# The opening of a two-layer SSM and GeGLU kernel: tap channels split 448 to 128 between TensorE and VectorE, D turned from one row, and two loads placed later

## Chip, cores and metric

The kernel runs on one core of one Trainium2 chip. The metric is the device time of one execution in microseconds (us). The kernel before takes 909.18 us, the median of three runs (909.0 to 909.36).

## What is computed

Four residual stages run over 2048 tokens of 576 channels: a gated convolution block (A), a GeGLU block (B), and the same two again with the same weights. All inputs are bf16.

```python
def _A_ref(q, k, v, shift_k, ssm_k, ssm_D):
    # k_shift: a causal convolution of k over 4 tokens, each channel with its 4 taps
    for t in range(ks):
        k_shift = k_shift + k_pad[:, t:t + S, :] * shift_k[:, ks - 1 - t][None, None, :]
    kv = k_shift * v
    # y: a causal convolution of kv over all 2048 tokens, each channel with its own filter ssm_k
    y = y + kv * ssm_D[None, None, :]
    return q * y

def _B_ref(x, w_gate, w_up, w_down):
    return (_gelu(x @ w_gate) * (x @ w_up)) @ w_down

x = A_q
x = x + _A_ref(_layernorm(x), A_k, A_v, A_shift_k, A_ssm_k, A_ssm_D)
x = x + _B_ref(_layernorm(x), B_w_gate, B_w_up, B_w_down)
x = x + _A_ref(_layernorm(x), ...)
x = x + _B_ref(_layernorm(x), ...)
```

## The kernel before

Tokens go in four blocks of 512, each held as 128 partitions by 4 rows (token 4p + i lies in partition p, row i). The long convolution is done block by block in a frequency domain: a block of kv is multiplied by tables of cosines and sines (W) on TensorE, the result (kc) is multiplied by the transformed filter (h0 and H) on VectorE, and the products (yb) go back through TensorE (L415). The term kv * D is folded into the filter: D is added to the filter's token 0. The GeGLU block streams its weights: wgu holds gate and up columns, wd the down rows, hT the hidden values. Its matmuls (L1743 and L1777) fill most of the time; the first of them, on half blocks, are at L1661.

All instructions are put out in an order written by hand or by a planner that runs at build time, and each engine works through its own list in that order. DMAs are issued from the lists of SP, ScalarE (ACT) and POOL; a DMA that waits holds up whatever is behind it in that list.

The function begin is the opening, for block 0. Around the change it does the following.

- sk9 and dv9 are the taps and D, loaded with 9 partitions of 64 channels each. L896 turns the taps into columns (wcol), L902 and L904 make diagonal matrices dg from them. L908 spreads the taps of the last 64 channels over all partitions (sx).
- L890 are matmuls on constants, eleven in all, before k has landed. L914 shifts the last three rows of k by one partition for the last 64 channels (kx).
- L922 turns k, four tiles of 128 channels (db 0 to 3, in two PSUM tiles, pts), and ScalarE copies them to kT (L927). shift_taps (L818) multiplies kT by the diagonals: fourteen matmuls for a pair of tiles. VectorE multiplies the result by v (L976).
- The remaining 64 channels (rest) are done by VectorE, multiply and add by tap (L938 to L944).
- L923 turns dv9, L931 copies it to dcol, and POOL adds dcol to the filter hn (L934). turn_h (L953) turns the filter, two of four rows at a time, rows 3 and 2 before the first taps and rows 1 and 0 before the second; L954 copies to hT0. Row 0 holds the token to which D is added.
- Then even and odd (L228) transform the filter, kfwd (L219) transforms v, apart (L233) and kacc (L359 to L362) are VectorE's work on both, straight (L415) is the way back, and the norm statistics of x stand between them. The transposes at L1461 and the copies at L1468 bring the normed x to the matmuls of L1661.
- POOL: taps_out writes the taps to DRAM as one row (skT) and loads k of block 1. At L1054 it loads that row into every partition as skc, the tap rows with which VectorE does the taps of blocks 1 to 3 (L194, L199, L204). At L1073 it loads v of block 1. Both are 576 KB. stats(3), the statistics of row 3, end with two POOL operations (L1484 and L1485). After them POOL works on L1229 and L1230 (norms), the stores of Hd and Kd (L425), additions by DMA (L389) and the loads of x_b (L1191) and kr (L547).
- SP loads, in this order: k, hn, v, W, x_b, Wx, W, the four turned pieces hx, wgu 0, the store Td, wgu 1 and wgu 2, hT1 (L966), and then three tiles of wd (L1186).

In first_half, L1667 is VectorE's multiplication of a hidden tile, and turn0 (L1461) turns rows 1 and 3 of x between the matmuls.

Of the kernel before, what the change touches and what calls it, by code (L numbers as in the profile page):

```python
# [15 lines left out]
ACT = mybir.ActivationFunctionType  # L16
ALU = mybir.AluOpType
F32 = mybir.dt.float32
BF16 = mybir.dt.bfloat16
# [3 lines left out]
P = 128  # L23
# [3 lines left out]
RT = BS // P  # L27
# [59 lines left out]
class Conv:  # L87
# [743 lines left out]
    def begin(self, head, tables):  # L831

        tc, nc, D, KS = self.tc, self.nc, self.D, self.KS
        nd = D // P
        width = lambda db: min(P, D - db * P)
        with ExitStack() as es:
            tmp = es.enter_context(tc.tile_pool(name="s_tmp", bufs=1))
            HP = P // 2
            NH = D // HP
            sk9 = tmp.tile([NH, 2, HP * KS], BF16, name="sk9")  # L840
            dv9 = tmp.tile([NH, 2, HP], BF16, name="dv9")
            sk9t = tmp.tile([NH, KS, HP], BF16, name="sk9t")
            hx = tmp.tile([P, RT, D], BF16, name="hx")
            dcol = tmp.tile([P, nd + 1], F32, name="dcol")
            nt = nd
            DW = D - nt * P
            wcol = tmp.tile([P, nt, KS], F32, name="wcol")
            sx = tmp.tile([P, KS, DW], BF16, name="sx")
            warm = tmp.tile([P, 1], F32, name="warm")
            self.Wx = tmp.tile([P, 2, P], BF16, name="Wx")  # L850
            Wn = tmp.tile([P, 2, P], BF16, name="Wn")
            hn = tmp.tile([P, nd + 1, BS], BF16, name="hn")
            hT0 = tmp.tile([P, RT, D], BF16, name="hT0")
            kT = head.scratch([P, nt, RT, P + 2], "kT")
            dg = head.scratch([P, nt, RT, P], "dg")
            kx = tmp.tile([P, RT + KS - 1, DW], BF16, name="kx")
            below = tmp.tile([P, P], BF16, name="below")
            wx = [tmp.tile([P, RT, DW], BF16, name=f"wx{i}") for i in range(2)]
            full = wx[1][:].rearrange("p i c -> p (i c)")[:, 0:256]

            twice = lambda src: src.unsqueeze(1).to_broadcast([NH, 2, src.shape[1]])
            nc.vector.memset(full, 1.0)
            nc.scalar.dma_start(out=sk9[:], in_=twice(self.sk.rearrange("(b p) j -> b (p j)", p=HP)))
            self.load_k(0, nc.sync)
            nc.scalar.dma_start(out=dv9[:], in_=twice(self.sD.rearrange("(b p) -> b p", p=HP)))
            nc.vector.memset(kT[:, :, :, 0:2], 0.0)
            nc.vector.memset(below[:, 0:1], 0.0)
            nc.vector.tensor_copy(out=below[:, 1:P], in_=self.ident[:, 0:P - 1])
# [16 lines left out]
            new_t = lambda: self.psp.tile([P, 2, 1024], BF16, tag="pr", name="pt")  # L885
            small_t = lambda: self.cpsp.tile([P, 2, 1024], BF16, tag="cps", name="cpt")

            def busy(ps, n):
                for _ in range(n):
                    nc.tensor.matmul(ps[:, 0, 0:256], lhsT=full[:, 0:P], rhs=full, start=True, stop=True)  # L890
            idle = small()
            busy(idle, 8)
            ps = new()
            halves = ((0, HP), (HP, P))
# [3 lines left out]
                nc.vector.tensor_copy(out=wcol[lo:hi], in_=ps[lo:hi, 0, 0:2 * nt * KS].rearrange("p (j b h) -> p b j h", b=nt, h=2)[:, :, :, h])  # L898

            def diagonals(db, js=range(KS)):  # L900
                for j in js:
                    nc.vector.tensor_scalar(out=dg[:, db, j, :], in0=self.ident[:], scalar1=wcol[:, db, j:j + 1], scalar2=None, op0=ALU.mult)  # L902
            for j in range(2):
                nc.scalar.activation(out=dg[:, nt - 1, j, :], in_=self.ident[:], func=ACT.Copy, scale=wcol[:, nt - 1, j:j + 1])  # L904
            for db in range(nt - 1):
                diagonals(db)
            ps = new()
            nc.tensor.matmul(ps[:, 0, 0:DW * KS], lhsT=self.ident[0:NH, NH - 1:NH].to_broadcast([NH, P]), rhs=sk9[:, 0, :], start=True, stop=True)  # L908
            nc.scalar.copy(out=sx[:], in_=ps[:, 0, 0:DW * KS].rearrange("p (d j) -> p j d", j=KS))
            busy(idle, 3)  # L910
            k, v = self.kt_[0], self.vt_[0]
            rest = slice(nt * P, D)
            px = new()
            nc.tensor.matmul(px[:, 0, 0:(KS - 1) * DW], lhsT=below[:], rhs=k[:, RT - KS + 1:RT, rest], start=True, stop=True)  # L914
            DBS = [(0, 1), (2, 3)]
            pts = []
            for n, dbs in enumerate(DBS):
                pt = new_t() if n else small_t()
                pts.append(pt)
                for e, db in enumerate(dbs):  # L920
                    for u in range(RT):
                        nc.tensor.transpose(pt[:, e, u * P:(u + 1) * P], k[:, u, db * P:(db + 1) * P], self.ident[:])  # L922
            nc.tensor.transpose(pt[:, 1, RT * P:RT * P + NH], dv9[:].rearrange("b h p -> b (h p)"), self.ident[0:NH, 0:NH])  # L923
            nc.scalar.copy(out=kx[:, 0:KS - 1, :], in_=px[:, 0, 0:(KS - 1) * DW].rearrange("p (i c) -> p i c", c=DW))
            for dbs, pt in zip(DBS, pts):
                ne = len(dbs)
                nc.scalar.copy(out=kT[:, dbs[0]:dbs[-1] + 1, :, 2:P + 2],  # L927
                               in_=pt[:, 0:ne, 0:RT * P].rearrange("p e (u q) -> p e u q", u=RT))
            for h, (lo, hi) in enumerate(halves):
                nb = (NH + 1 - h) // 2  # L930
                nc.scalar.copy(out=dcol[lo:hi, 0:nb], in_=pts[1][lo:hi, 1, RT * P + h:RT * P + NH:2])  # L931

            for lo, hi, w in ((0, nd, P), (nd, nd + 1, D - nd * P)):
                nc.gpsimd.tensor_tensor(out=hn[0:w, lo:hi, 0], in0=hn[0:w, lo:hi, 0], in1=dcol[0:w, lo:hi], op=ALU.add)  # L934

            tt = nc.vector.tensor_tensor
            tap = lambda j: sx[:, j, :].unsqueeze(1).to_broadcast([P, RT, DW])
            tt(out=wx[0][:], in0=k[:, 0:RT, rest], in1=tap(0), op=ALU.mult)  # L938
            nc.vector.tensor_copy(out=kx[:, KS - 1:, :], in_=k[:, 0:RT, rest])
            diagonals(nt - 1, range(2, KS))  # L940
            for j in range(1, KS):
                tt(out=wx[1][:], in0=kx[:, KS - 1 - j:KS - 1 - j + RT, :], in1=tap(j), op=ALU.mult)
                tt(out=wx[0][:], in0=wx[0][:], in1=wx[1][:], op=ALU.add)
            tt(out=v[:, :, rest], in0=wx[0][:], in1=v[:, :, rest], op=ALU.mult)  # L944

            def turn_h(pt, g):

                hv = hn[:].rearrange("p b (q i) -> p b i q", i=RT)
                for dbs in (range(nd), (nd,)):
                    for i in (2 * g + 1, 2 * g):  # L950
                        for db in dbs:
                            w = width(db)
                            nc.tensor.transpose(pt[:, i % 2, db * P:db * P + w], hv[0:w, db, i, :], self.ident[0:w, 0:w])  # L953
                nc.scalar.copy(out=hT0[:, 2 * g:2 * g + 2, :], in_=pt[:, :, 0:D])  # L954

            def taps_of(dbs, ps):
                o = ps[:].rearrange("p e (i c) -> p e i c", i=RT)
                for e, db in enumerate(dbs):
                    self.shift_taps(k, kT, dg, P, db, o[:, e])
                return o  # L960
            out = []
            for n, dbs in enumerate(DBS):
                turn_h(new_t(), 1 - n)
                out.append(taps_of(dbs, new() if n else small()))
            self.hT1 = head.scratch([P, RT, D], "hT1")[:]
            nc.sync.dma_start(out=self.hT1, in_=self.Td[1].rearrange("(p i) d -> p i d", i=RT))  # L966
            skT = tc.dram_tile([1, KS * D], BF16, name="skT")

            def taps_out():
                nc.gpsimd.tensor_copy(out=sk9t[:], in_=sk9[:, 0, :].rearrange("b (p j) -> b j p", j=KS))  # L970
                nc.gpsimd.dma_start(out=skT[:].rearrange("o (j b p) -> (o b) j p", j=KS, p=HP), in_=sk9t[:])
                self.load_k(1, nc.gpsimd)
            for dbs, o in zip(DBS, out):
                ne = len(dbs)
                vd = v[:, :, dbs[0] * P:(dbs[0] + ne) * P].rearrange("p i (e c) -> p e i c", e=ne)
                tt(out=vd, in0=o[:, 0:ne], in1=vd, op=ALU.mult)  # L976

            h0, kc, A, E = {}, {}, {}, {}
            self.H1 = head.stay()
# [21 lines left out]
            def kfwd(kt, s, ps):  # L1001
                if s == 0:
                    kc[kt] = self.kcp.tile([P, 2, D], BF16, tag="kc", name="kc")
                self.fwd_full(v, kt, s, kc[kt], ps=ps)
# [6 lines left out]
            def kacc(kt):  # L1011
                for part in range(2):
                    t = self.ybp.tile([P, D], BF16, tag="yb", name="yb")
                    self.prod(part, kc[kt], h0[kt], t[:])
                    A[(part, kt)] = t
# [35 lines left out]
            head.scales(0)  # L1051
            head.scales(2)
            kacc(0)
            nc.gpsimd.dma_start(out=self.skc[:].rearrange("p j d -> p (j d)"), in_=skT[:].broadcast_to([P, KS * D]))  # L1054
            kfwd(2, 0, small())
            kfwd(2, 1, new())
            even(1, 0)
# [12 lines left out]
            kfwd(3, 0, small())  # L1070
            head.even_out(2)
            kfwd(3, 1, new())
            self.load_v(1, nc.gpsimd)  # L1073
            head.act_stats(1)
            Y = {mt: new() for mt in (0, 2)}
            for kts in ((0, 2), (1,)):
# [26 lines left out]
            nc.scalar.activation(out=warm[:], in_=head.zero, func=ACT.Gelu_apprx_tanh)  # L1103
            self.keep_y(0, 3, Y[3])
            head.stats(3)
            head.gate(1, None, 0)
            self.A0 = A

# [762 lines left out]
```

## Time and profile before

| | us |
|---|---|
| runs, median (lowest to highest) | 909.18 (909.0 to 909.36) |
| the profiled execution | 909.58 |
| its span, first to last instruction | 907.8 |

Durations below come from this one profiled execution; it took 0.4 us more than the median, and 1.78 us of it lie outside the span. PE is TensorE's matmul, PEld its weight load, DVE VectorE, ACT ScalarE, SP the sync engine, whose list holds most DMA issues. Busy times of the engines in four stretches of the opening:

| stretch, us | PE | DVE | ACT | POOL | share of the DMA engines | GB/s |
|---|---|---|---|---|---|---|
| 0 to 13.4 | 11.78 | 8.15 | 7.93 | 1.03 | 0.92 | 286 |
| 13.4 to 28 | 14.12 | 13.91 | 12.10 | 8.13 | 1.04 | 272 |
| 28 to 34.5 | 5.82 | 5.68 | 4.00 | 0.00 | 1.07 | 284 |
| 34.5 to 50 | 15.37 | 14.76 | 10.45 | 10.15 | 1.10 | 304 |

The granted TensorE clock was 1.00 throughout. [...] Where an engine waited for several things, the profile names the one that came last, and that is an inference.

### The profile page before, as it was taken

How to read it: one execution, taken by the hardware profiler on the slowest of the kernel's cores; microseconds unless marked ns; L12 is line 12 of the kernel's file. 1: busy time of each engine (PE TensorE's matmuls, PEld its weight loads, DVE VectorE, ACT ScalarE, POOL GpSimd, SP SyncE). 2: the span in 40 equal slices, each digit the busy share in tenths (PEclk: the TensorE clock that was granted, in tenths of full speed). 3: DMA queues.
4: the chain of work that ended last, by engine and by line, in shares of the span. 5: the costliest groups of instructions: out<-in, count | busy, mean ns of one | idle time of the engine just before them, and what ended most of it. 6: DMA issues, size and time to landing. Idle time of an engine off the chain costs nothing.

```text
span 907.8 us, 19177 instructions
## 1 busy us (share of the span) xinstructions
PE 901.5 (99%) x8142; PEld 524.8 (58%) x8142; DVE 575.2 (63%) x988; ACT 328.3 (36%) x614; POOL 157.8 (17%) x336
## 2 busy tenths in 40 slices
PE   9999999999999999999999999999999999999998
PEld 6875646556466465564654655645646546556555
DVE  7989977688889884787898855443332335333332
ACT  6765455423222254443115133551121124321211
POOL 3324315120213031420104002310000003100000
PEclk9999999999999999999999999999999999999999
DMA  9999997766429319675815601961620621967620
GB/s 272 305 294 284 257 264 124 188 194 151 167 68 264 93 22 179 211 139 133 272 54 132 170 4 41 195 129 39 126 73 14 145 80 27 190 160 173 142 57 27
DMA packets 132076, 132.91 MB, mean 146 GB/s; under 512 B 46139, under 2 KB 123670, under 8 KB 131990
## 3 DMA queue, kind: packets, MB, share of 16 engines
q1 hardware_dynamic: 121728, 94.65, 46.5%
q0 software_dynamic: 10208, 37.02, 12.9%
q8 instruction: 63, 1.03, 0.5%
q14 instruction: 23, 0.19, 0.1%
q10 hardware_dynamic: 54, 0.01, 0.0%
HBM read 108.36 MB, written 12.39 MB: 133 GB/s over the span
## 4 chain that ended last, share of the span: by engine, by line
PE 96%; DVE 2%; DMA 1%; issue 0%; DVEq 0%; SPq 0%
PE gu L1743 59%; PE dn L1777 31%; PE gu L1661 2%; DMA hT<-Td 1%; PE cps L282 1%; PE ps L415 1%; PE ps L282 0%; PE cps L415 0%; DVE yb L362 0%; DVE prod L359 0%; DVE h L233 0%; DVE prod L361 0%; PE cps L890 0%; DVE hT L1667 0%; DMA out_dram<-ob 0%; PE cps L818 0%
## 5 line engine op out<-in xcount | busy, mean ns | idle before, releaser
L1743 PE MATMUL gu<-xnT,wgu 64*128 64x512 bf16 x4968 | 540.7, 376 | 0.0
L1743 PEld LDWEIGHTS <-wgu 64*128 64x128 bf16 x4968 | 239.7, 94 | 294.4 <-issue 6.2
L1752 ACT ACTIVATE ga<-gu 128x512 f32<-128x512 f32 x258 | 153.9, 597 | 450.9 <-PE gu L1743 442.5
L1753 DVE TENSOR_TENSOR hT<-ga,gu 128x512 bf16<-128x512 f32 x258 | 177.1, 686 | 200.4 <-ACT ga L1752 198.9
L1777 PE MATMUL dn<-wd,hT 128*128 128x288 bf16 x2304 | 292.1, 286 | 0.0
L1777 PEld LDWEIGHTS <-hT 128*128 128x128 bf16 x2304 | 223.5, 98 | 65.6 <-issue 9.5
L1816 DVE TENSOR_TENSOR x_c<-x_c,dn 128x576 f32<-128x576 f32 x62 | 46.7, 753 | 55.3 <-PE dn L1777 54.9
L1214 POOL TENSOR_SCALAR nm<-s 128x1 f32<-128x1 f32 x56 | 20.1, 359 | 264.5 <-DVE x_c L1808 210.8
L1222 ACT ACTIVATE junk<-x_c,nm 128x576 bf16<-128x576 f32 x48 | 36.9, 769 | 28.4 <-POOL nm L1214 25.9
L555 POOL DMA_DIRECT2D hr<-Hd x32 | 17.5, 547 | 118.5 <-DVE prod L361 117.9
L1230 POOL TENSOR_TENSOR rstd<-ve,neghalf_t 128x1 f32<-128x1 f32 x58 | 36.9, 636 | 4.8
L1286 ACT ACTIVATE xn<-x_c,nb,rstd 128x576 bf16<-128x576 f32 (+1 forms) x48 | 28.6, 644 | 5.9 <-POOL nb L1234 5.7
L1229 POOL TENSOR_SCALAR ve<-ss 128x1 f32<-128x1 f32 x58 | 21.9, 377 | 47.0 <-ACT junk L1222 46.9
L1799 DVE TENSOR_TENSOR ob<-x_c,dn 128x576 bf16<-128x576 f32 x15 | 11.3, 754 | 29.1 <-PE dn L1777 28.3
L285 ACT COPY eo<-cps 128x576 f32<-128x576 f32 x29 | 18.7, 643 | 27.3 <-PE cps L282 24.1
L1640 ACT ACTIVATE ga<-gu 128x512 bf16<-128x512 f32 x26 | 15.5, 598 | 30.5 <-PE gu L1743 25.9
L1661 PE MATMUL gu<-xnT,wgu 64*128 64x256 bf16 x432 | 24.9, 269 | 0.6 <-ACT xnT L1468 0.6
L1661 PEld LDWEIGHTS <-wgu 64*128 64x128 bf16 x432 | 21.4, 94 | 3.5 <-issue 1.4
L362 DVE TENSOR_TENSOR prod<-prod 128x576 bf16<-128x576 bf16 x48 | 22.0, 458 | 1.6
L430 POOL DMA_DIRECT2D out_dram<-ob x12 | 6.8, 564 | 91.7 <-DVE ob L1799 91.7
L245 DVE SCALAR_TENSOR_TENSOR eo<-eo 128x576 f32<-128x576 f32 x22 | 16.3, 753 | 5.8 <-ACT eo L285 5.8
L1264 DVE SCALAR_TENSOR_TENSOR x_c<-g_t,rstd,x_c 128x576 f32<-128x576 f32 x16 | 13.0, 815 | 8.7 <-POOL rstd L1230 8.7
(182 smaller groups left out, 588.7 us busy)
## 6 DMA issues: line engine op xcount, KB each, us to landing
wgu<-in_B_w_gate_dram SPq DMA_DIRECT2D x45, 576.0 KB, 5.8
wd<-in_B_w_down_dram SPq DMA_DIRECT2D x30, 864.0 KB, 6.7
wgu<-in_B_w_up_dram SPq DMA_DIRECT2D x45, 512.0 KB, 8.0
hr<-Hd POOLq DMA_DIRECT2D x32, 288.0 KB, 4.7
kr<-Kd POOLq DMA_DIRECT2D x24, 288.0 KB, 4.8
Kd<-kc POOLq DMA_DIRECT2D x12, 288.0 KB, 6.0
k<-in_A_k_dram POOLq DMA_DIRECT2D x3, 1008.0 KB, 11.7
wgu<-in_B_w_up_dram SPq DMA_DIRECT2D x45, 64.0 KB, 7.5
```

Source lines behind the costliest of these rows:

```text
L362: nc.vector.tensor_tensor(out=dst, in0=pr[:, 0, :], in1=pr[:, 1, :], op=ALU.subtract if part == 0 else ALU.add)
L1214: nc.gpsimd.tensor_scalar(out=v["nm"][:], in0=v["s"][:], scalar1=-1.0 / D, scalar2=None, op0=ALU.mult)
L1222: nc.scalar.activation(out=junk[:], in_=get_x(), func=ACT.Square, bias=v["nm"][:, 0:1], accum_out=v["ss"][:])
L1229: nc.gpsimd.tensor_scalar(out=ve[:], in0=v["ss"][:], scalar1=1.0 / D, scalar2=EPS, op0=ALU.mult, op1=ALU.add)
L1230: nc.gpsimd.tensor_tensor(out=v["rstd"][:], in0=ve[:], in1=neghalf_t[:, 0:1], op=ALU.pow)
L1286: nc.scalar.activation(out=xn[:, lo:hi], in_=x_c[c][:, j, 0:hi - lo], func=ACT.Identity, scale=v["rstd"][:, 0:1], bias=v["nb"][:, 0:1])
L1661: nc.tensor.matmul(pair[:, s, e * 256:(e + 1) * 256], lhsT=w[r0:r0 + HK, k, gi * P:(gi + 1) * P], rhs=xnT[r0:r0 + HK, blk_of[k], tok], sta ...
L1743: nc.tensor.matmul(pair[:, s, :], lhsT=w[r0:r0 + HK, k, gi * P:(gi + 1) * P], rhs=xnT[r0:r0 + HK, b, :], start=(k == 0), stop=(k == NKC - 1))
L1752: nc.scalar.activation(out=ga[:], in_=pair[:, 0, :], func=ACT.Gelu_apprx_tanh)
L1753: nc.vector.tensor_tensor(out=hT[:, fi, :], in0=ga[:], in1=pair[:, 1, :], op=ALU.mult)
L1777: nc.tensor.matmul(part[h][:, h, 0:HW], lhsT=hT[:, fi, at * P:(at + 1) * P], rhs=wd[2 * wb + fi // WT][:, fi % WT, h * HW:(h + 1) * HW], s ...
L1816: nc.vector.tensor_tensor(out=xh, in0=xh, in1=acc[:, :, 0:HW], op=ALU.add)
```

## The change

It has three parts. First, VectorE takes 128 channels instead of 64 (DW), and TensorE 448 instead of 512: its fourth tile is 64 wide (tw gives a tile's width). With it, sx needs two matmuls, kx is 128 wide, the copies of kT and the multiplications by v are three instructions instead of two, and one of the eleven matmuls on constants goes. Second, D is loaded as one row of 576 (dvec), and turned by five one-column transposes (turn_d) that stand behind the turn of filter rows 3 and 2; the copies to dcol and POOL's additions move there too. Third, the loads of skc and of v of block 1 move from the middle of the opening to behind stats(3). After the opening every engine's order is as before.

```diff
-            dv9 = tmp.tile([NH, 2, HP], BF16, name="dv9")
+            dvec = tmp.tile([1, D], BF16, name="dvec")
...
-            DW = D - nt * P
+            DW = P
+            tw = lambda db: min(P, D - DW - db * P)
...
-            nc.scalar.dma_start(out=dv9[:], in_=twice(self.sD.rearrange("(b p) -> b p", p=HP)))
+            nc.scalar.dma_start(out=dvec[:], in_=self.sD.unsqueeze(0))
...
             def diagonals(db, js=range(KS)):
+                w = tw(db)
                 for j in js:
-                    nc.vector.tensor_scalar(out=dg[:, db, j, :], in0=self.ident[:], scalar1=wcol[:, db, j:j + 1], scalar2=None, op0=ALU.mult)
+                    nc.vector.tensor_scalar(out=dg[0:w, db, j, 0:w], in0=self.ident[0:w, 0:w], scalar1=wcol[0:w, db, j:j + 1], scalar2=None, op0=ALU.mult)
...
-            nc.tensor.matmul(ps[:, 0, 0:DW * KS], lhsT=self.ident[0:NH, NH - 1:NH].to_broadcast([NH, P]), rhs=sk9[:, 0, :], start=True, stop=True)
+            for c in range(DW // HP):
+                nc.tensor.matmul(ps[:, 0, c * HP * KS:(c + 1) * HP * KS],
+                                 lhsT=self.ident[0:NH, NH - DW // HP + c:NH - DW // HP + c + 1].to_broadcast([NH, P]),
+                                 rhs=sk9[:, 0, :], start=True, stop=True)
...
-            busy(idle, 3)
+            busy(idle, 2)
...
-            rest = slice(nt * P, D)
+            rest = slice(D - DW, D)
...
-                        nc.tensor.transpose(pt[:, e, u * P:(u + 1) * P], k[:, u, db * P:(db + 1) * P], self.ident[:])
-            nc.tensor.transpose(pt[:, 1, RT * P:RT * P + NH], dv9[:].rearrange("b h p -> b (h p)"), self.ident[0:NH, 0:NH])
+                        nc.tensor.transpose(pt[0:tw(db), e, u * P:(u + 1) * P], k[:, u, db * P:db * P + tw(db)], self.ident[:])
...
-            for dbs, pt in zip(DBS, pts):
-                ne = len(dbs)
-                nc.scalar.copy(out=kT[:, dbs[0]:dbs[-1] + 1, :, 2:P + 2],
-                               in_=pt[:, 0:ne, 0:RT * P].rearrange("p e (u q) -> p e u q", u=RT))
-            for h, (lo, hi) in enumerate(halves):
-                nb = (NH + 1 - h) // 2
-                nc.scalar.copy(out=dcol[lo:hi, 0:nb], in_=pts[1][lo:hi, 1, RT * P + h:RT * P + NH:2])
-
-            for lo, hi, w in ((0, nd, P), (nd, nd + 1, D - nd * P)):
-                nc.gpsimd.tensor_tensor(out=hn[0:w, lo:hi, 0], in0=hn[0:w, lo:hi, 0], in1=dcol[0:w, lo:hi], op=ALU.add)
-
+            for lo, hi, w, pt in ((0, 2, P, pts[0]), (2, 3, P, pts[1]), (3, 4, tw(3), pts[1])):
+                nc.scalar.copy(out=kT[0:w, lo:hi, :, 2:P + 2],
+                               in_=pt[0:w, lo % 2:lo % 2 + hi - lo, 0:RT * P].rearrange("p e (u q) -> p e u q", u=RT))
+
+            def turn_d(pt):
+
+                at = RT * P
+                for db in range(nd + 1):
+                    w = width(db)
+                    nc.tensor.transpose(pt[0:w, 1, at + 2 * db:at + 2 * db + 1], dvec[:, db * P:db * P + w], self.ident[0:1, 0:1])
+                for lo, hi, w in ((0, nd, P), (nd, nd + 1, D - nd * P)):
+                    nc.scalar.copy(out=dcol[0:w, lo:hi], in_=pt[0:w, 1, at + 2 * lo:at + 2 * hi:2])
+                    nc.gpsimd.tensor_tensor(out=hn[0:w, lo:hi, 0], in0=hn[0:w, lo:hi, 0], in1=dcol[0:w, lo:hi], op=ALU.add)
...
-            def turn_h(pt, g):
+            def turn_h(pt, g, first=None):
...
+                if first:
+                    first()
                 nc.scalar.copy(out=hT0[:, 2 * g:2 * g + 2, :], in_=pt[:, :, 0:D])
...
-                    self.shift_taps(k, kT, dg, P, db, o[:, e])
+                    self.shift_taps(k, kT, dg, tw(db), db, o[:, e])
...
-                turn_h(new_t(), 1 - n)
+                turn_h(new_t(), 1 - n, None if n else lambda: turn_d(pts[1]))
...
-            for dbs, o in zip(DBS, out):
-                ne = len(dbs)
-                vd = v[:, :, dbs[0] * P:(dbs[0] + ne) * P].rearrange("p i (e c) -> p e i c", e=ne)
-                tt(out=vd, in0=o[:, 0:ne], in1=vd, op=ALU.mult)
+            for lo, hi, o in ((0, 2, out[0]), (2, 3, out[1]), (3, 4, out[1])):
+                w = tw(lo)
+                vd = v[:, :, lo * P:(hi - 1) * P + w].rearrange("p i (e c) -> p e i c", c=w)
+                tt(out=vd, in0=o[:, lo % 2:lo % 2 + hi - lo, :, 0:w], in1=vd, op=ALU.mult)
...
             kacc(0)
-            nc.gpsimd.dma_start(out=self.skc[:].rearrange("p j d -> p (j d)"), in_=skT[:].broadcast_to([P, KS * D]))
             kfwd(2, 0, small())
...
             kfwd(3, 1, new())
-            self.load_v(1, nc.gpsimd)
             head.act_stats(1)
...
             head.stats(3)
+            nc.gpsimd.dma_start(out=self.skc[:].rearrange("p j d -> p (j d)"), in_=skT[:].broadcast_to([P, KS * D]))
+            self.load_v(1, nc.gpsimd)
             head.gate(1, None, 0)
```

More of the change, by code (lines that the diff above doesn't have):

```diff
@@ L900, in diagonals @@
             def diagonals(db, js=range(KS)):
+                w = tw(db)
                 for j in js:
-                    nc.vector.tensor_scalar(out=dg[:, db, j, :], in0=self.ident[:], scalar1=wcol[:, db, j:j + 1], scalar2=None, op0=ALU.mult)
+                    nc.vector.tensor_scalar(out=dg[0:w, db, j, 0:w], in0=self.ident[0:w, 0:w], scalar1=wcol[0:w, db, j:j + 1], scalar2=None, op0=ALU.mult)
             for j in range(2):
-                nc.scalar.activation(out=dg[:, nt - 1, j, :], in_=self.ident[:], func=ACT.Copy, scale=wcol[:, nt - 1, j:j + 1])
+                w = tw(nt - 1)
+                nc.scalar.activation(out=dg[0:w, nt - 1, j, 0:w], in_=self.ident[0:w, 0:w], func=ACT.Copy, scale=wcol[0:w, nt - 1, j:j + 1])
             for db in range(nt - 1):
```

## The prediction

> **What bounds the kernel now.** I read first the page's busy shares and chain by line, then the opening in the timelines of TensorE, VectorE, ScalarE and POOL, then the chain of waits up to 65 us, and last the DMA queues in short windows.
>
> ```profile
> PE 901.5 (99%) x8142; PEld 524.8 (58%) x8142; DVE 575.2 (63%) x988; ACT 328.3 (36%) x614; POOL 157.8 (17%) x336
> PE gu L1743 59%; PE dn L1777 31%; PE gu L1661 2%; DMA hT<-Td 1%; PE cps L282 1%; PE ps L415 1%; PE ps L282 0%; PE cps L415 0%; DVE yb L362 0%; DVE prod L359 0%; DVE h L233 0%; DVE prod L361 0%; PE cps L890 0%; DVE hT L1667 0%; DMA out_dram<-ob 0%; PE cps L818 0%
> ```
>
> TensorE is busy for 901.5 of 907.8 us, so a change to the opening can win only the few idle stretches there and the matmuls that it drops. The timelines (start, length, engine, line, tile, count, and in brackets the idle time before with its releaser) show the stretches:
>
> ```profile
> 10.16 1.92 PE L818 MATMUL ps<-dg,kT 128*128 128x512 bf16 x14
> 13.39 1.14 PE L219 MATMUL cps<-v,W 128*128 128x288 bf16 x8 [0.34 <-DVE v L976]
> ...
> 28.13 0.90 PE L415 MATMUL ps<-yb,W 128*128 128x288 bf16 x6 [0.62 <-DVE yb L362]
> ...
> 34.51 8.11 PE L1661 MATMUL gu<-xnT,wgu 64*128 64x256 bf16 x144 [0.56 <-ACT xnT L1468]
> ```
>
> ```profile
> 8.40 0.29 DVE L944 TENSOR_TENSOR v<-wx,v 128x256 bf16<-128x256 bf16 x1
> 9.63 1.23 DVE L976 TENSOR_TENSOR v<-cps,v 128x1024 bf16<-128x1024 f32 x1 [0.94 <-PE cps L818]
> 12.11 1.23 DVE L976 TENSOR_TENSOR v<-ps,v 128x1024 bf16<-128x1024 f32 x1 [1.25 <-PE ps L818]
> ...
> 44.02 0.75 DVE L194 TENSOR_TENSOR kvt<-k,skc 128x1152 bf16<-128x1152 bf16 x1
> 44.69 0.68 DVE L1667 TENSOR_TENSOR hT<-ga,gu 128x512 bf16<-128x512 f32 x1
> ```
>
> TensorE taps end at 12.09; VectorE multiplies v (12.11 to 13.35); only then can the transform of v (L219) start. From 13.4 to 28 VectorE is busy for 13.9 of 14.6 us and the chain runs along it, so what the opening wins before 13.4 travels on to the dense matmuls at 34.51, and from there to the end, because TensorE hardly idles afterwards. The chain (start, length, what) has one more place:
>
> ```profile
> 29.61 10.10 DMA hT<-Td
> ...
> 44.10 0.67 DVE kvt L194
> 44.77 0.61 DVE hT L1667
> 45.42 0.66 PE xps L1461 x9
> ```
>
> The DMA step is an inference: that issue has no landing in the list of issues, and VectorE idled only 0.22 us there. What I keep is the end of it: L194, the first reader of the tap rows skc, stands directly ahead of L1667, and L1667 ahead of the transposes at 45.42. A late skc is paid in full.
>
> **The change, part by part.** I carry the old times forward.
>
> *TensorE before the taps.* From 4.39 (k lands 3.6 us after its issue at 0.74; one warming matmul less and one L908 more before that are hidden by this wait) it runs without a gap. L914 doubles from 192 columns (0.32 us): L219 takes 0.12 for 288 columns and L890 0.234 for 256, so 0.08 to 0.17 more; I take 0.10. The turn of D at L923 leaves (0.12 in the chain). Five turns of one column come behind the first ten of L953: at 0.063 each (ten in 0.63 at 9.60) to 0.12 (L923), 0.32 to 0.60; I take 0.35, by the warm row. They write the bank that ScalarE's copies of kT read, and wait for ScalarE: sx and kx double (0.35 and 0.32 us become about 0.56 and 0.45), which fits into the 0.54 us that ScalarE idles before 5.60; then come 0.96 for four blocks, 0.52 for one and 0.52 for the 64-row one, to about 7.7, so 0.06 of waiting. Behind these turns queue the first taps: they end at 9.60 + 0.10 - 0.12 + 0.35 + 0.06 = 9.99.
>
> *ScalarE and POOL.* The two copies of dcol (0.33 together) now wait for the turns, with the hT0 copy behind them (7.82 becomes about 8.45, ended 9.6); its reader L228 runs at 11.91. POOL's addition of D (0.34) goes from 7.88 to about 8.5 and is needed by L953 near 10. Both cost nothing under the first taps (1.88 us); without that cover 0.6.
>
> *VectorE's channels.* The nine instructions of L938 to L944 go from 256 to 512 elements a row. Bf16 products take 0.29 for 256, 0.46 for 576 and 0.75 for 1152, so about 0.43: 8 x 0.13 for products and sums, 0.05 for the copy, 0.05 back for smaller diagonals. VectorE ends this at 8.69 + 1.04 = 9.73, ahead of 9.99: free. At twice 0.29 each it would end at 11.0 and push the first L976.
>
> *The taps.* Block 3 has 64 channels: its seven matmuls fall from 2048 to 1024 columns. Fourteen take 1.88 us for 4096, so 0.94 becomes 0.52, with 0.063 as the floor of the short ones: -0.42. The second taps end at 9.99 + 0.63 + 1.86 - 0.42 = 12.06. The L976 product behind them (1.23 for 1024 elements, 0.75 for 576, so 1.07 ns each) is now 512 and 256 elements, 0.68 + 0.41 - 0.06 of overlap = 1.03: end 13.10 instead of 13.35. **Gain 0.25 us**; with the upper prices (turns 0.60, L914 0.17) a loss of 0.07, with the lower ones and 0.5 for the taps a gain of 0.4.
>
> *The loads that move.* skc and v of block 1, 576 KB each, leave POOL's queue at 22.34 and 24.64 and go behind the statistics of row 3:
>
> ```profile
> 22.34 0.63 POOL L1054 DMA_DIRECT2D skc<-skT  x1
> 24.64 0.54 POOL L181 DMA_DIRECT2D v<-in_A_v_dram  x1 [1.67 <-PE ps L219]
> ...
> 35.98 0.97 POOL L1485 TENSOR_TENSOR rstd<-ve,neghalf_t 128x1 f32<-128x1 f32 x1
> 38.64 0.71 POOL L1229 TENSOR_SCALAR ve<-ss 128x1 f32<-128x1 f32 x1 [1.69 <-ACT junk L1222]
> ```
>
> The issue starts at 36.97 and both are out by 38.2, under the idle 1.69 before L1229; if they took 0.8 more each, L1229, L1230 and the norm at 40.31 would follow up to 0.7 late. skc has from 36.97 to 44.02, **7.05 us**, whatever the opening wins, since both ends move together. Durations to landing:
>
> ```profile
> v<-in_A_v_dram POOLq DMA_DIRECT2D x1, 576.0 KB, 4.0
> ...
> x_b<-in_A_q_dram POOLq DMA_DIRECT2D x1, 576.0 KB, 7.8
> ...
> skc<-skT POOLq DMA_DIRECT2D x1, 576.0 KB, 8.3
> ```
>
> The first, at 184.88, meets engines that are 40% busy; the second, at 155.55, runs beside a weight load and moves nothing until 160; the third stood behind k (1008 KB, 11.7). So 4.0 to 8.8 (v behind skc). Which row is nearest hangs on what SP's queue holds at 37:
>
> ```profile
> q0 software_dynamic: 430, 2.20, 69.0%
> q1 hardware_dynamic: 927, 0.90, 35.3%
> ...
> q1 hardware_dynamic: 1062, 1.10, 109.9%
> ```
>
> From 22 to 32 POOL's queue (q0) moved 2.20 MB and SP's (q1) 0.90; from 32 to 37 SP's alone moved 1.10, 0.22 MB a microsecond. With 1.18 of those 2.20 MB gone, SP's backlog (the third wgu, then hT1 at 37 to 39) is through some 3 to 4 us sooner, near 35.5, and the wd loads still start at 36.04. So skc meets a queue that is just filling: I take 6 us, landing at 43.0, **no stall**, and v some 2 us later, needed at 50.04 by L204. The stores of Hd and Kd and the kr loads behind them on POOL (39.93 to 54.75) shift by up to 3 us; kr is read at 82.33 and the next x_b at about 79, so this is covered by more than 15 us.
>
> [...]
>
> **Sum.** 907.8 - 0.25 = 907.55 span. This execution took 909.58, 1.78 more than its span and 0.4 above the median of the three runs (909.18), so the median becomes 909.18 - 0.25 = **908.9**.
>
> **Rivals.** (A) skc lands late and its wait takes VectorE: L194, L1667 and the transposes at 45.42 slip by the excess over 7.05. It decides from 7.3 us on, where the opening's gain is eaten. At 7.8: 0.75 - 0.25, 909.7; at 8.8: 1.75 - 0.25, 910.7; at k's 11.7: 913.6. For it: three loads of this size on POOL in the crowded stretch took 8.1 to 8.8. Against: each stood behind another on its queue, and here the queue is empty. (B) The opening wins nothing, because the single-column turns or the doubled VectorE work cost their upper prices: 909.2. (C) The idle stretches at 13.05, 28.13 and 34.51 close too, as loads no longer crowd that stage: 1.5 us, with the 0.25 about 907.4; against it, every one of them is put down to VectorE or ScalarE, none to a transfer.
>
> **Chances.** Forecast 0.51, A 0.31 (0.15 of it above 911.0, that is a landing after some 9.1 us), B 0.11, C 0.07. 0.2% of 909.2 is 1.8 us, about what a measurement of this kernel can tell from no change: faster 0.07 (C), slower 0.15, within 0.78. The forecast's own range is 908.7 to 909.3 by the two prices of the opening; the range over the cases, 907.9 to 911.2, leaves out C and most of A's far part.
>
> **What would show it.** Right: L976's last piece ends near 13.1, L219 follows at once, POOL issues skc near 36.7, and L194 starts near 43.8 without a DMA as its releaser. Wrong: VectorE idle before L194 put down to skc, with an equal gap of TensorE near 45; turns of D over 0.5 us; VectorE's channels ended after 10. A time under 907.4 would mean that a transfer held TensorE in the old kernel without the trace saying so.

## The result and the profile after

| | before | after |
|---|---|---|
| median, us (lowest to highest, runs) | 909.43 (909.0 to 909.56, 6) | 912.74 (911.88 to 915.85, 6) |
| profiled execution, us | 909.58 | 912.63 |
| its span, us | 907.8 | 910.9 |

The ratio is 1.0041, 95% interval 1.0026 to 1.0056: slower, where no measurable change was forecast, and above the forecast range of 907.9 to 911.2. From here on line numbers are those of the kernel that is spoken of; in the kernel after, L953 has become L960, L976 L985, L1054 L1113, L1186 L1195, L1461 L1470, L1661 L1670 and L1667 L1676.

The 3.1 us of span fall in two places. Where nothing waits, TensorE's work behind the opening comes in the same order and at the same distances in every trace of this study, so the shift of a landmark (the start of a given group of matmuls) against the kernel before gives a loss of the profiled execution to 0.01 us. The dense matmuls (L1661, now L1670) start at 36.09 instead of 34.51, **1.58 us late**. From the transposes at L1470 on everything is 3.07 to 3.08 us late, so another **1.50 us** lie between. Nothing is added later.

The first loss, in TensorE's timeline of the kernel after (start, length, engine, line, tile, count):

```profile
6.66 1.26 PE L960 MATMUL pt<-ident,hn 128*128 128x128 bf16 x10
7.87 0.38 PE L939 MATMUL pt<-ident,dvec 1*128 1x1 bf16 x5
8.19 3.60 PE L818 MATMUL cps<-dg,kT 128*128 128x512 bf16 x14
11.57 0.88 PE L960 MATMUL pt<-ident,hn 128*128 128x128 bf16 x10
12.39 1.59 PE L818 MATMUL ps<-dg,kT 128*128 128x512 bf16 x14
```

The first fourteen taps take 3.60 us, against 1.92 to 1.94 in the kernel before. It is no wait: they run without a gap, each at half the pace. The ten turns ahead of them take 1.26 and the same ten behind them 0.88. By the starts of the single matmuls, 128 columns take 107 ns up to about 11.7 us and 56 ns from then on; in the kernel before the pace doubles near 7.7. The granted clock reads 1.00 in both only because the profile counts as 1.00 the time for which the trace has no entry of the clock. The first entry, of 1.00, starts at 11.74 us in the kernel after and at 7.75 in the kernel before, so its start is the date of the doubling. All dates below are these starts; one trace (e5) has no entry, and its date is read from the matmuls.

The second loss, in VectorE's timeline of the kernel after, with the idle time and its releaser in brackets:

```profile
9.35 0.43 DVE L951 TENSOR_TENSOR v<-wx,v 128x512 bf16<-128x512 bf16 x1
11.82 1.23 DVE L985 TENSOR_TENSOR v<-cps,v 128x1024 bf16<-128x1024 f32 x1 [2.05 <-PE cps L818]
14.02 1.02 DVE L985 TENSOR_TENSOR v<-ps,v 128x512 bf16<-128x512 f32 x2 [0.97 <-PE ps L818]
...
47.09 0.76 DVE L194 TENSOR_TENSOR kvt<-k,skc 128x1152 bf16<-128x1152 bf16 x1 [1.41 <-DMA skc<-skT]
47.76 0.68 DVE L1676 TENSOR_TENSOR hT<-ga,gu 128x512 bf16<-128x512 f32 x1
```

L194 now waits 1.41 us for skc, L1676 stands behind it, and the chain of waits of the kernel after goes through the load:

```profile
38.47 8.53 DMA skc<-skT
46.99 0.03 issue
47.02 0.02 DVEq L194
47.05 0.04 issue
47.09 0.76 DVE kvt L194
47.85 0.61 DVE hT L1676
48.45 0.04 issue
48.50 0.66 PE xps L1470 x9
```

TensorE has the equal gap there (1.61 us idle ahead of L1470). What moved meanwhile, by the DMA queues of the kernel after in the windows 37 to 39, 39 to 41, 41 to 42.5, 42.5 to 44 and 44 to 47 us (packets, MB, share of the engines, a sum of packet times that q1 nearly alone takes to 107.5%; q1 is SP's queue, q0 POOL's):

```profile
q1 hardware_dynamic: 24, 0.04, 13.0%
...
q1 hardware_dynamic: 471, 0.54, 82.0%
...
q1 hardware_dynamic: 519, 0.58, 107.5%
q0 software_dynamic: 3, 0.01, 2.2%
...
q1 hardware_dynamic: 235, 0.27, 53.9%
q0 software_dynamic: 69, 0.32, 52.4%
...
q0 software_dynamic: 163, 0.67, 62.2%
q1 hardware_dynamic: 161, 0.19, 24.8%
```

POOL issues skc at 38.47, with the DMA engines nearly idle. SP has issued two of its three wd tiles by then (864 KB each, 1.77 MB together, at 37.62 and 38.05) and issues the third at 38.64. SP's packets flow first, 1.1 MB of them. POOL's queue starts at 42.42, 3.95 us after the issue, and from 44 us on the two go on packet for packet.

### The profile page after: what moved, and what is told of

Read it like the earlier page. It is cut to its first block, busy times and chain, and to the rows that moved or that the text cites. A ratio compares the mean times of both kernels' runs of the same rounds, so it can differ in the third digit from the quotient of the medians.

```text
span 910.9 us, 19187 instructions
## 1 busy us (share of the span) xinstructions
PE 903.4 (99%) x8146; PEld 525.4 (58%) x8146; DVE 576.0 (63%) x989; ACT 328.7 (36%) x615; POOL 157.4 (17%) x336
## 3 DMA queue, kind: packets, MB, share of 16 engines
q8 instruction: 63, 1.03, 0.5%
## 4 chain that ended last, share of the span: by engine, by line
PE 96%; DVE 2%; DMA 1%; issue 0%; POOL 0%; DVEq 0%
PE gu L1752 59%; PE dn L1786 31%; PE gu L1670 2%; DMA skc<-skT 1%; PE cps L282 1%; PE ps L415 1%; PE cps L415 1%; PE ps L282 0%; DVE yb L362 0%; DMA k<-in_A_k_dram 0%; PE cps L818 0%; DVE prod L359 0%; DVE h L233 0%; DVE prod L361 0%; PE pt L960 0%; PE ps L228 0%
## 5 line engine op out<-in xcount | busy, mean ns | idle before, releaser
L1238 POOL TENSOR_SCALAR ve<-ss 128x1 f32<-128x1 f32 x58 | 21.8, 376 | 46.1 <-ACT junk L1231 45.9
L1670 PE MATMUL gu<-xnT,wgu 64*128 64x256 bf16 x432 | 24.9, 269 | 0.6 <-ACT xnT L1477 0.6
L1670 PEld LDWEIGHTS <-wgu 64*128 64x128 bf16 x432 | 21.4, 94 | 3.5 <-issue 1.4
L194 DVE TENSOR_TENSOR kvt<-k,skc 128x1152 bf16<-128x1152 bf16 x24 | 17.9, 754 | 1.7 <-DMA skc<-skT 1.4
```

What stands on the lines that cost most here:

```text
L1238: nc.gpsimd.tensor_scalar(out=ve[:], in0=v["ss"][:], scalar1=1.0 / D, scalar2=EPS, op0=ALU.mult, op1=ALU.add)
L1670: nc.tensor.matmul(pair[:, s, e * 256:(e + 1) * 256], lhsT=w[r0:r0 + HK, k, gi * P:(gi + 1) * P], rhs=xnT[r0:r0 + HK, blk_of[k], tok], sta ...
```

## Experiments

Each kernel was run beside the kernel before on the same chip; medians of before were 909.90 (first four), 910.58, 910.23, 910.13 and 909.98 in the five batches. The landmark is the start of the dense matmuls, 34.51 in the kernel before. "Stall" is how much later than in the kernel before the transposes of L1461 come behind that start. "Pace" is the date of the doubling. Landmark, stall and pace belong to the one profiled execution of each kernel.

**e1: the kernel after, loads back at their old places.**

```diff
             kacc(0)
+            nc.gpsimd.dma_start(out=self.skc[:]..., in_=skT[:].broadcast_to([P, KS * D]))
...
             kfwd(3, 1, new())
+            self.load_v(1, nc.gpsimd)
...
             head.stats(3)
-            nc.gpsimd.dma_start(out=self.skc[:]..., in_=skT[:].broadcast_to([P, KS * D]))
-            self.load_v(1, nc.gpsimd)
```

> The changed kernel with both loads (skc, v of block 1) back at their old places; the new opening stays. Theory: two losses that add up, 1.6 us before 13.4 us, because TensorE's transposes and taps run at 107 ns for 128 columns until 11.7 us (before: until 7.4 us), and 1.5 us at 48.5 us, where skc is late. Then this kernel keeps the first loss alone: 911.0, no DMA wait at L194, the dense matmuls start near 36.1 instead of 34.5. Rival, the loads are the whole loss and the slow taps of the profiled run were chance: 909.0 to 909.4, dense matmuls at 34.3.

Measured: 910.75, ratio 1.0015 (0.9997 to 1.0034). No stall; pace doubled at 10.16, dense matmuls at 35.36, 0.85 late.

**e2: the kernel before with the loads at the new place** (the same edit the other way round).

> The kernel before with the two loads at their new place and nothing else. Theory of two losses: dense matmuls at 34.5 as before, VectorE waits about 1.4 us for skc (landing 8.5 us after its issue at 37.0, so near 45.5), TensorE stands still about 1.5 us near 45.4, total 910.9. Rival, the opening is the whole loss and the stall is given back later: 909.4.

Measured: 912.35, ratio 1.0023 (1.0014 to 1.0033). Pace at 7.20, dense matmuls at 34.38, stall 0.90; skc issued at 36.76 and landed 7.9 us later. VectorE's line:

```profile
44.78 0.76 DVE L194 TENSOR_TENSOR kvt<-k,skc 128x1152 bf16<-128x1152 bf16 x1 [0.81 <-DMA skc<-skT]
```

The moved loads lose by themselves. The profiled execution (910.32) was the fastest of ten, so its stall of 0.90 does not account for the whole loss of the median.

**e3: e1 with D as nine rows, turned the old way. e4: e1 with the third constant matmul back** (busy(idle, 3)).

> The changed kernel with the loads back and D again turned as nine rows in one transpose ahead of the filter rows, its copies ahead of hT0; the 448 to 128 split and the ten constant matmuls stay. If the five one-column turns and the waits around them keep TensorE at the slow pace for another stretch, the pace doubles near 7.4 us again and the total is 909.2 (the opening wins its 0.25). If the split itself or the missing constant matmul does it, it stays near 911.0.

> The changed kernel with the loads back and eleven matmuls on constants instead of ten, as before; the turns of D stay new. If the missing constant matmul ahead of the landing of k is what delays the faster pace, the pace doubles near 7.4 us and the total is 909.2. If the one-column turns or the split do it, 911.0.

Measured: e3 909.79, 1.0005 (0.9994 to 1.0015), pace at 9.06, dense matmuls at 34.65. e4 909.71, 0.9991 (0.9962 to 1.0021), pace at 7.27, dense matmuls at 34.38. Both lost less than e1, and in both the pace doubled sooner; one profile each could not tell which part was the reason. In e4 TensorE also waits 0.89 and 0.29 us near 152 us for a transposed load (xnT), and in e10 0.83 us; the change touches nothing there, and no run tests these waits. TensorE's timeline of e4, at about the pace that the kernel before had, shows the opening nearly as forecast:

```profile
7.91 0.35 PE L939 MATMUL pt<-ident,dvec 1*128 1x1 bf16 x5
8.19 1.92 PE L818 MATMUL cps<-dg,kT 128*128 128x512 bf16 x14
9.95 0.80 PE L960 MATMUL pt<-ident,hn 128*128 128x128 bf16 x10
10.68 1.59 PE L818 MATMUL ps<-dg,kT 128*128 128x512 bf16 x14
```

**e5: e2 with skc issued from ScalarE's list. e9: the same, but behind ScalarE's first L1666.** The edit of e5 against the kernel before, without the two lines that go at the old places:

```diff
             head.stats(3)
+            nc.scalar.dma_start(out=self.skc[:]..., in_=skT[:].broadcast_to([P, KS * D]))
+            self.load_v(1, nc.gpsimd)
```

> The kernel before with both loads at the new place, as in e2_loads_only, but skc issued from ScalarE's list and only v from POOL's. Theory one, the delay belongs to POOL's queue (its first packets went out 3.5 us after the issue in the kernel after, and then shared the engines one packet for one with SP's): skc lands 3 to 5 us after its issue, as k does in the opening from SP's list (3.6), L194 starts without a DMA as its releaser, the dense matmuls at L1661 and the transposes at L1461 stand 11 us apart as before (34.51 and 45.42), and the time is 909.0 to 910.2 beside 909.9 for the kernel before. Theory two, the wd loads and the other traffic from 39 us on fill the DMA engines and any queue would be as late: skc lands 7 us or more after its issue, L194 waits for it 0.5 to 2 us, and the time is 910.5 to 913. The issue itself takes ScalarE some 0.6 us (0.59 for sk at 0.73 us), which may move its copies at L1468 by as much.

> As e5_skc_scalar_queue (skc from ScalarE's list, v from POOL's, the rest the kernel before), but skc is issued behind ScalarE's first copy of L1666, at about 36.6 us: the moment at which POOL issued it in e2_loads_only (36.76), where e5 issued it at 33.64. Theory one, POOL's queue is what is slow (first packet 4.1 us after the issue in e2): skc's first packets go out by 39, it lands by 42.5 (within 6 us of its issue), L194 starts near 43.9 without waiting for it, time 909.5 to 910.3. Theory two, in e5 the earlier issue was the cure: skc's first packets come some 4 us after this issue as well, it lands at 44 to 46, and L194 waits 0.5 to 2 us for it: time 910.5 to 912.5.

Measured: e5 909.48, 0.9991 (0.9971 to 1.0011), no stall. But ScalarE had issued skc at 33.64, ahead of the wd tiles (35.84), so the run could not tell the queue from the time of issue. In e5 too skc's first packet came 3.91 us after its issue, behind 0.95 MB of loads that SP had issued before it, and the first wd packet only at 38.95. e9 put the issue at 37.56, behind the first two wd tiles (36.78 and 37.21): 913.14, 1.0022 (1.0004 to 1.0040), stall 1.62, landing 8.7 us after the issue:

```profile
46.37 0.76 DVE L194 TENSOR_TENSOR kvt<-k,skc 128x1152 bf16<-128x1152 bf16 x1 [1.52 <-DMA skc<-skT]
```

POOL's queue is not what is slow. The queues of e9 from 38 to 41 us and from 41 to 43 (q10 is ScalarE's):

```profile
q1 hardware_dynamic: 762, 0.87, 90.3%
...
q10 hardware_dynamic: 74, 0.34, 44.1%
q1 hardware_dynamic: 246, 0.27, 38.7%
q0 software_dynamic: 44, 0.20, 25.7%
```

and of e5 from 38 to 39 us, where skc goes while the wd tiles wait:

```profile
q10 hardware_dynamic: 93, 0.39, 94.0%
q1 hardware_dynamic: 14, 0.02, 6.3%
```

**e13: e2 with SP's wd loads held back until skc and v are issued.**

```diff
         d = dpool.tile([P, WT, D], BF16, tag="wd", name="wd")
+        if n == 0:
+            nc.gpsimd.memset(d[:, 0, 0:1], 0.0)
         nc.sync.dma_start(out=d[:], in_=B_w_down[r0:r0 + WT * P, :]...)
```

> The kernel before with both loads at the new place on POOL, as in e2_loads_only, and the three wd loads of SP held back until skc and v have been issued: POOL writes one column of the first wd tile behind them, and SP's first wd load waits for that, so it is issued at about 38.1 us instead of 35.9. Theory three, the engines serve loads in the order of their issue, and skc was late because the first wd tile (864 KB, issued 0.9 us ahead of it) went first: skc's first packets come by 39, it lands by 41.5 (under 5 us), L194 does not wait, and the time is 909.4 to 910.4. Theory four, any load needs some 4 us to its first packet at this point whatever stands ahead of it: first packets at 40.5 to 41, and from there it shares the engines with wd, landing at 43 to 45; L194 waits up to 1 us, time 910.3 to 912.

The queues of e13 from 36.5 to 37.5 us, 37.5 to 39 and 39 to 41, and the issues from 36 to 42 us with the time to landing:

```profile
q1 hardware_dynamic: 68, 0.25, 81.5%
...
q0 software_dynamic: 75, 0.35, 68.8%
q1 hardware_dynamic: 10, 0.03, 4.6%
...
q0 software_dynamic: 129, 0.52, 94.1%
...
wd<-in_B_w_down_dram SPq DMA_DIRECT2D x3, 864.0 KB, 18.3
skc<-skT POOLq DMA_DIRECT2D x1, 576.0 KB, 4.4
```

skc, issued at 36.51, has its first packet at 37.86, 1.35 us later, and lands after 4.4; no stall. A fixed delay of 3.9 us, which the other runs would have allowed, is excluded by that. Now the wd tiles wait: issued from 37.82 on, they have their first packet at 41.40, 3.58 us later. In these runs it is the order of issue that counts. The bill comes elsewhere: the wd tiles land 18.3 us after their issue, SP's next wgu loads, issued from 52.45 us on, stand behind them, and TensorE's timeline of e13 shows two stops:

```profile
102.02 10.45 PE L1779 MATMUL dn<-wd,hT 128*128 128x288 bf16 x84 [0.82 <-DMA wd<-in_B_w_down_dram]
117.75 18.19 PE L1745 MATMUL gu<-xnT,wgu 64*128 64x512 bf16 x143 [4.96 <-DMA wgu<-in_B_w_up_dram]
```

Behind the second stop the clock's entry reads 0.50 from 116.0 to 122.8 us, and the matmuls of 512 columns start 427 ns apart until 122.8 and 216 from then on, which costs some 2.5 us more (an estimate: half of the 5.1 us from 117.75 on). This shows once more that the clock's entries date the pace. The run takes 918.38 (median of four), ratio 1.0089 (1.0055 to 1.0123); the only forecast of theory three that failed was its time.

**e10: the kernel before with v alone at the new place.**

> The kernel before with only v of block 1 at the new place, skc where it was. v lands by 46 at the latest and is first read at L204 near 50 us, so both theories have no wait in this stretch: dense matmuls at 34.2 to 34.6, transposes at L1461 near 45.4 and 909.4 to 910.3, the time of the kernel before. A theory by which the crowd on POOL's queue behind v (Hd, yb, kr) is what costs the 2 us would have 911 or more.

Measured: 910.67, 1.0009 (0.9995 to 1.0022), no stall, dense matmuls at 34.52: v late costs nothing here, and the stall is skc's.

**The opening: e6, the kernel before with two constant matmuls ahead of k; e7, the kernel after with three; e8, e3 with three; e11, the kernel before with nine and two; e12, the kernel after again; e14, the kernel before with none; e15, with five; e16 is e6 again, e17 e14, e18 e8.**

```diff
-            busy(idle, 8)
+            busy(idle, 9)
...
-            busy(idle, 3)
+            busy(idle, 2)
```

(e11; the others change one of these numbers.)

> The kernel before with one constant matmul less ahead of k (two after the spread of the taps instead of three), nothing else. Theory one, TensorE's pace doubles later when the stretch ahead of k holds less full-width work: matmuls of 128 columns keep 107 ns beyond 8.5 us, the first taps take 2.4 to 3.6 us instead of 1.9, and the dense matmuls start 0.5 to 1.6 us after the 34.51 of the kernel before; time 910.4 to 911.5. Theory two, the new work of the opening is what slows it (nine-row and one-column matmuls, ScalarE's wait): the pace doubles at 7.3 to 7.5 as before, dense matmuls at 34.3 to 34.6, time 909.9.

> The kernel after with the third constant matmul back. Theory one (the missing constant matmul delays the pace): the pace doubles at 7.3 to 7.5, the second taps end near 12.2, the dense matmuls start at 34.3 to 34.5 instead of 36.09, so 1.6 to 1.8 us come back, and the stall at L194 stays or grows by what it had been shortened: 910.2 to 912.0 beside 912.7 for the kernel after. Theory two (the one-column turns of D hold the pace down): the pace doubles after 9 us, the dense matmuls start after 35.2, and the time stays at 912 to 913.

> The 448 to 128 split alone: loads at their old places, D as nine rows turned the old way, three constant matmuls. Both theories have the pace double at 7.3 to 7.5. Against e4_fill_three, which differs only in the turn of D (dense matmuls at 34.38), this gives the price of the five one-column turns with their wait: if they cost the 0.3 to 0.6 us that TensorE spends between 7.58 and 8.20 in e4 against some 0.3 in e3, the dense matmuls start near 34.1, 0.4 sooner than in the kernel before (34.51); if the turns lie beside something that sets the end anyway (VectorE's channels, ended near 9.8), near 34.4. Time 909.3 to 909.9.

> The kernel before with one constant matmul moved, not dropped: nine in the first group and two ahead of k, eleven in all as before. Theory one, the idle time of TensorE just ahead of k (0.25 to 0.4 us with three, 0.5 with two) is what puts off the doubling of the pace: it comes at 9 to 11.7 us as in the four kernels with two, and the dense matmuls start 0.5 to 1.6 us after 34.51. Theory two, the amount of full-width work ahead of k counts, wherever it stands: the doubling comes at 5.1 to 7.9 as in the six kernels with three, dense matmuls at 34.2 to 34.7.

> The kernel after once more, unchanged, for a second sample of the two losses. Theory one: the pace doubles between 9.0 and 11.7 us, so the dense matmuls start 0.5 to 1.6 us after 34.51; skc's first packets come 3.5 to 4.2 us after its issue, it lands 7.9 to 8.8 us after it, and L194 waits 0.8 to 1.8 us. Rival: the loss at one of the two places was an accident of the one profile, the pace doubles before 8, or L194 does not wait. Time 911.5 to 913.5.

> The kernel before without any of the three constant matmuls ahead of k, so that TensorE idles some 0.9 us there. If the work of this stretch sets when the pace doubles, it comes at 8.5 to 11.8 us as in the kernels with two, the dense matmuls start at 34.7 to 36.1, and the time is 0.4 to 1.6 us above the kernel before. If the spread among the kernels with two and three is chance (two: 8.5 to 11.7, three: 5.2 to 8.9), it can come as early as 5.2, and the dense matmuls start near 34.4.

> The kernel before with five constant matmuls ahead of k instead of three, so that TensorE does not idle there (it starts on k some 0.1 to 0.2 us late). If the work of this stretch sets when the pace doubles, it comes at 5.0 to 8.5 us and the dense matmuls start at 34.2 to 34.8; if chance, anything between 5.2 and 11.7 and up to 36.

> The kernel of e6_two_fills once more. If two constant matmuls ahead of k really put off the doubling of TensorE's pace (all five kernels with two so far: 8.5 to 11.7 us), it comes after 8.4 again and the dense matmuls start at 34.6 to 36.1. If the five were chance, the odds are for 7.3 to 7.9, where nine of the twelve others lie, and for dense matmuls at 34.3 to 34.6.

> The kernel of e14_no_fills once more (pace doubled at 7.7, dense matmuls at 34.71). If less work ahead of k puts it off and that 7.7 was a lucky phase, 8.4 to 11.8 and dense matmuls at 35.0 to 36.3. If the work ahead of k does not matter, 5.2 to 7.9 again and 34.3 to 34.8.

> The kernel of e8_d_old_three_fills once more, in more rounds: the 448 to 128 split without the other parts, which is the best version that the runs point to. The dense matmuls start 0.2 to 0.4 us ahead of the 34.51 of the kernel before if the pace doubles before 8 us, L194 does not wait, and the ratio lies between 0.9985 and 1.0005; a pace that doubles after 8.5 would take the gain away.

| constant matmuls ahead of k | full pace from, us (dense matmuls against 34.51) |
|---|---|
| two, old work | e6 10.12 (+1.19), e16 8.88 (+0.59) |
| two, new work | after 11.74 (+1.58), e12 8.08 (+0.15), e1 10.16 (+0.85), e3 9.06 (+0.14) |
| three, old work | before 7.75, e2 7.20 (-0.13), e5 5.1 (-0.19), e9 8.90 (+0.74), e10 7.44 (+0.01), e13 6.76 (-0.38) |
| three, new work | e4 7.27 (-0.13), e7 5.21 (-0.40), e8 7.90 (-0.28), e18 9.64 (+0.44) |
| none, old work | e14 7.58 (+0.20), e17 7.95 (+0.14) |
| five; nine and two, old work | e15 7.37 (+0.08); e11 7.38 (+0.09) |

The times agree in direction but are too scattered to decide: e6 911.01 (ratio 1.0005, 0.9986 to 1.0023), e16 910.71 (1.0017, 0.9990 to 1.0043), e14 910.44, e17 910.36, e11 910.34, e15 909.85, e8 909.79 and e18 910.75 (1.0003, 0.9979 to 1.0027) are all within their intervals of no change. e7 took 911.98 (1.0026, 1.0010 to 1.0043) with stall 1.35, e12 913.11 (1.0039, 1.0016 to 1.0062) with stall 1.80.

e6 looked like proof that the missing constant matmul puts the doubling off. e14 and e17 speak against so simple a rule: with none it came at 7.58 and 7.95. The date also moves from run to run of one kernel: 11.74 and 8.08, 10.12 and 8.88, 7.90 and 9.64. The six with two (and ten in all) are the later ones on average (9.7 against 7.4 for the other fourteen), but they overlap with three (8.90, 9.64). So it is shown that the date of the doubling decides most of what the opening loses; the rest is the landing of k, since TensorE starts on k between 4.33 (e13) and 4.72 us (e12).

What sets the date is not shown: neither the number of constant matmuls nor the change's own work gives it by itself, and the two traces of the kernel after lie 3.66 us apart (11.74 and 8.08). So whether the change makes the doubling late stays open; of the four traces with the new work and two constant matmuls, two doubled after 10 us (11.74, 10.16) and two sooner (9.06, 8.08).

In e12, the same kernel as after, the first taps ran at full pace and skc cost more:

```profile
8.19 0.35 PE L939 MATMUL pt<-ident,dvec 1*128 1x1 bf16 x5
8.47 1.92 PE L818 MATMUL cps<-dg,kT 128*128 128x512 bf16 x14
```

The split alone with three constants (e8, e18), v alone moved (e10) and skc issued early from ScalarE's list (e5) are clear of the stall, but no version is measurably faster than the kernel before.

## Why the prediction was wrong

**Opening, "gain 0.25 us": its working held within its bounds, its pace did not.** VectorE's channels were to end at 9.73 and ended at 9.78. The five one-column turns were priced at 0.35 and took 0.32 (7.87 to 8.19). The L976 product was to take 1.03 and took 1.02. In e4, at about the old pace, the first taps end at 10.11, by the sum 9.99, and the second at 12.27, by the sum 12.06: L914 cost 0.16 more where 0.10 was taken, and the fourth block saved 0.33 where 0.42 was taken. The dense matmuls start 0.13 us earlier in e4, half of the forecast; e8, without the one-column turns, has 0.28. The step that failed is the one that carried durations of TensorE forward from the old trace (fourteen taps in 1.88) as if they belonged to the instructions. They belong to the pace of that moment: the taps took 3.60. The warning stood in the old profile: the same 128 columns took 107 ns at 7.1 us and 56 ns at 8.2. The price of the date shows best in e6 and e16, one kernel whose first taps start at 7.71 both times: each microsecond by which the doubling comes later costs (35.70 - 35.10) / (10.12 - 8.88) = 0.48 us. "One warming matmul less ... hidden by this wait" was right about the wait, but it put the matmul's price in pace at nothing; no run settles that price: with two of them the pace doubled at 9.7 us on average, in the other fourteen traces at 7.4, and the ranges overlap. The opening of one kernel lost 1.58 in this execution, with the doubling at 11.74, and 0.15 in e12, with the doubling at 8.08.

**Loads, "I take 6 us, landing at 43.0, no stall": mis-sized by 2 to 3 us.** skc took 8.5 us (8.8 in e12, 7.9 in e2) of the 7.05 it had. That SP's backlog would be gone held: its queue used 13% of the engines from 37 to 39. But "skc meets a queue that is just filling" counted the packets that move and not the loads that had been issued: the prediction itself had wd at 36.04 and skc at 36.97, and the two tiles (1.77 MB) issued up to 0.9 us ahead are what skc waits behind: 1.1 MB went before its first packet. e13 turns the order round and has 4.4 us.

**Rival A was the right one in mechanism and close in price** (8.8 us: 1.75 late; measured 1.50 at 8.5 and 1.80 at 8.8), and "paid in full" held: 1.41 us of VectorE, 1.50 of TensorE. The argument against it, that skc's own queue was empty, fell with e9: the queue does not matter. Rival C fell: the 0.62 us ahead of L415 stayed (at 29.71). Rival B needed the upper prices of the opening; L914 came near its own (0.16 of 0.17), the turns and VectorE's channels did not.

**The edits costed at nothing** were so: POOL's two issues fit under its wait (L1238 at 40.22, still released by ScalarE), v landed 10.2 us after its issue without a reader waiting, and e10 confirms it.

The account of the profiled run closes: 1.58 + 1.50 = 3.08 of 3.1 us. The medians do not split so well: the loads alone lose 2.45 us (e2 against its kernel before), the whole change 3.31 (e12 2.88). The 0.4 to 0.9 left for the opening is smaller than these intervals can tell from nothing, and so is e1, the opening alone (1.0015, 0.9997 to 1.0034).

## What to carry to other kernels

When a load is moved, list what the other engines issue in the microseconds ahead of it and add up its bytes; an idle stretch of the DMA engines and an empty queue of its own did not make it first here (13.0% and an empty POOL queue, and 1.1 MB of SP's went ahead). Durations of matmuls from the first ten microseconds of a trace held here only for that pace (107 or 56 ns for 128 columns): read the starts of single matmuls and the first entry of the clock, and take a second profile before pricing anything there. Where runs scatter by 2 us, a landmark compares two profiled executions to 0.01 us; it says nothing of the other executions, as e2 shows.

## What was not expected of the hardware

Loads of different queues were served by the order of their issue at first: skc's first packet came 3.9 us after its issue on POOL's list (after 3.95, e2 3.95, e7 3.88, e12 3.87) and on ScalarE's (e9 3.86) alike when wd tiles stood ahead, in each case after 920 to 1000 packets (1.0 to 1.3 MB) of SP's. It came after 3.91 us in e5, behind earlier loads of SP's (0.95 MB), and after 1.35 us in e13, with only 0.27 MB of SP's ahead. From 44 to 47 us, with both queues flowing, packets went one for one (163 and 161); at the start SP's went ahead alone, and why some thousand packets is not shown.

TensorE's pace doubled between 5.1 and 11.7 us, 3.9 to 10.5 us after its first matmul. At 128 columns the pace went from 107 ns to 56 (before and after). The date varied from run to run of one kernel, 11.74 and 8.08 us in the kernel after; what sets it is not shown.
